# Attention with its normalisation moved from the exponentials to the product, and the reciprocals brought to rows through DRAM

## The chip, the cores and the metric

The kernel runs on one core of a Trainium2 chip. The metric is the device time of one execution in microseconds; lower is better. Five engines matter: TensorE (PE, with its weight loads PEld), VectorE (DVE), ScalarE (ACT), GpSimd (POOL), and SyncE (SP), whose queue issues nearly all transfers.

## The reference

Three stages follow each other. The first is causal attention with a decay over 4 batches of 8 heads, 576 rows and 64 columns; the change is in it. The other two are dense layers over 2304 tokens, 512 to 2048 to 512, with a swish and then a prelu.

```
scores = scale * q k^T + (cum_i - cum_j),  causal
attn = exp(scores - max(scores))
attn = attn / (sum(attn) + 1e-9)
x = attn v          # then [2304, 512]
h = x w_in;  g = h * sigmoid(1.702 h);  x = g w_out
h = x w2_in; g = max(h, 0) + alpha * min(h, 0);  out = g w2_out
```

## The kernel before

**Units.** Attention works on pairs of heads: 4 batches x 4 pairs. Each pair's 576 query rows are cut into a chunk of 256 rows (two tiles of 128) and one of 320 (two tiles of 128 and one of 64 that holds both heads), 32 chunks in all. `chunk` makes scores in PSUM, reduces and masks them on VectorE (L891) into `e`, and takes exponentials in place on ScalarE (L900), which also gives the row sums in `ms`. Then each tile adds 1e-9 to its sums (L905, L909), takes reciprocals (L911), and scales `e` in place by a per-row scalar (L917 on ScalarE, L919 on VectorE or GpSimd). `chunk2`, called one chunk later, transposes `e` on TensorE (L952), copies the transposes to `eT` (L513, L515), multiplies them with v (L966) into one PSUM buffer, and copies the product, which is transposed (columns are query rows), into the ring `xr` (L979). The PSUM pool for that product holds one buffer.

**Background.** The first dense layer (`gemm1`, L1008) works on blocks of 256, 320, 256, 320 and 384 rows as soon as all four pairs of heads have delivered their columns of `xr`; it needs `xh` and `xl`, the high and low parts of `xr`, and weights prepared on all engines. The last 768 rows go through `tail` (L1031). Its matmuls fill TensorE between the attention's.

**Order.** Nothing is ordered by the program's text. `Plan.plan` places all operations by a list schedule with costs and due times; `Plan.run` then emits them in planned order, so each engine's stream is fixed. In the plan a transfer takes 540 ns of its queue, ends 750 ns after a start-up of 1500 ns and its bytes, and its users may start after its `lag` on top of that. Operations of `back` (priorities 1000 to 2000, gemm1) carry a planned penalty if they could start, in nanoseconds the third number of `TRIES`; the first is the penalty for switching the matmul mode, within the second. In the first 130 us `Plan.run` puts filler matmuls on the identity (L484) where the plan leaves TensorE idle.

Of the kernel before, what the change touches and what calls it, by code (L numbers as in the profile page):

```python
# [7 lines left out]
F32 = mybir.dt.float32  # L8
# [4 lines left out]
ALU = mybir.AluOpType  # L13
# [14 lines left out]
TMODE = 0  # L28
PADC = 8000.0
PAD0, PAD1, PADN, PADM = 1600.0, 130000.0, 220.0, 200.0  # L30
TRIES = [(800.0, 3000.0, 200.0)]
QUEUE = {"SP": "SP", "ACTQ": "ACT"}


# [215 lines left out]
def kernel(  # L250
# [13 lines left out]
    nc = tc.nc  # L264

    B, H, S, D = q.shape
    NT, DM = out.shape
    DFF = w1_in.shape[1]
    P = 128
    BH = B * H  # L270
    NP = H // 2
# [12 lines left out]
    RING = 1152  # L284
    SPLIT = 256
# [16 lines left out]
    plan = Plan()  # L302
    E = {"PE": nc.tensor, "DVE": nc.vector, "ACT": nc.scalar, "POOL": nc.gpsimd, "SP": nc.sync, "ACTQ": nc.scalar}
# [3 lines left out]
    dram = ctx.enter_context(tc.tile_pool(name="dram", bufs=1, space=bass.MemoryType.DRAM))  # L307
# [4 lines left out]
    tscr = dram.tile([P, KEPT, WSLOT], F32, name="tscr")  # L312
    w2scr = dram.tile([P, NPAIR, WSLOT], F32, name="w2scr")
    cscr = dram.tile([BH, 2, S], F32, name="cscr")
    region = {}

    order_of = {
# [17 lines left out]
    def sb(reg, nm, slots, shape, dt=F32, after=()):  # L335
        p = Pool(slots, after)
        p.make = lambda i: open_region(reg).tile(shape, dt, name=f"{nm}{i}", tag=f"{nm}{i}")
        return p
# [45 lines left out]
    xr = region["p1"][1].tile([P, KT, RING], F32, name="xr")  # L384
    p1_pools = [p_xh, p_xl, p_gg, p_xr]

    att = region["att"][1]
# [4 lines left out]
    p_z = sb("att", "Z", 2, [P, 2, 2, 64], F32R)  # L392
    bm = att.tile([P, 2], F32, name="bm")
    p_raw = sb("att", "raw", 3, [P, S])
    p_tk = sb("att", "tk", 1, [P, S])

    p_ka = sb("att", "KA", 2, [P, 2, S], F32R)
    p_kb = sb("att", "KB", 2, [P, 1, S], F32R)
    p_qa = sb("att", "QA", QS, [P, 2, S], F32R)
    p_vr = sb("att", "VR", 2, [P, NKT, 2, D])  # L400
    p_ms = sb("att", "ms", 4, [P, 16])
    p_e0 = sb("att", "ea", 2, [P, 6 * P])
    p_e2 = sb("att", "eb", EB, [P, 2, 3 * P])
    p_e3 = sb("att", "ec", EB, [P, 2, 4 * P])
    p_e4 = sb("att", "ed", EB, [P, 5 * P])
    p_et = sb("att", "eT", ET, [P, 640])
    att_pools = [p_z, p_raw, p_tk, p_ka, p_kb, p_qa, p_vr, p_ms, p_e0, p_e2, p_e3, p_e4, p_et]

    banks = [psum.tile([P, 512], F32, name=f"bk{i}") for i in range(8)]

# [83 lines left out]
    lfT = lambda: xr[:, 0, RING - S - NKT * BH:RING - S].rearrange("p (t r) -> p t r", r=BH)  # L494

    b_id, b_mask, b_mask2, b_cum, b_alpha = Buf(), Buf(), Buf(), Buf(), Buf()
    DMA = lambda nbytes: [("SP", nbytes / 360.0)]

    def c_dve(n, fast=False):
        return n / (1.92 if fast else 0.96) + 68.0  # L500
# [10 lines left out]
    def copy(e, dst, src):  # L511
        if e == "ACT":
            nc.scalar.copy(dst, src)  # L513
        else:
            E[e].tensor_copy(dst, src)  # L515
# [10 lines left out]
    def a_out(n):  # L526
        return [("ACT", c_act(n, True)), ("DVE", c_dve(n), BC + WO_ * n)]
# [73 lines left out]
    every = slice(None)  # L601
# [10 lines left out]
    def filled(nm, p):  # L612
        return [fill[nm, len(p.bufs) - 1]] if len(p.bufs) <= p.n else []
# [8 lines left out]
    for part, (lo, hi) in enumerate(((0, SPLIT), (SPLIT, S))):  # L622
        ts_ = [t for t in range(NKT) if lo <= t * P < hi]
        pri = -80 if part == 0 else A0 + P1PRI
# [23 lines left out]
        cs = slice(lo, hi)  # L648
# [13 lines left out]
        [(b_cc, 0)],  # L662
        ("vr", p_vr, lambda x: x[64:P, NKT - 1], 2 * D, 0.0, every),
        ("ed", p_e4, lambda x: x[:, S:], 64, 0.0, every),
    )
    for i in range(2):
        set_rows("dk", p_kb, [i], lambda i=i: p_kb.tiles[i][:, 0], S, -40, [(b_cc, 0)], 0, 64)
# [165 lines left out]
    def a_scale(n):  # L833
        return [("DVE", c_dve(n, True) + 62.0, SC_D, True), ("ACT", c_act(n) + 105.0, SC_A), ("POOL", 280.0 + 2.55 * n, SC_P, True)]

    def chunk(u, q0, q1, pri):
        kh, kl, dk, qh, ql, qo, z = (u[x] for x in ("kh", "kl", "dk", "qh", "ql", "qo", "z"))
        pr = lambda c: range(2 if c > SPLIT else 1)
        ms = Buf(p_ms)
        n = q1 - q0  # L840
        tiles = [(t, t * P, min(P, S - t * P)) for t in range(q0 // P, (q1 + P - 1) // P)]
        view, eb = {}, {}
        if not q0:
            e0 = Buf(p_e0)
        for j, (t, a, w) in enumerate(tiles):
            ext = a + w
# [12 lines left out]
            step = ext if ext <= 512 else ext // 2  # L859
# [43 lines left out]
            last.clear()  # L903
            if w < P:
                plan.add([("DVE", 75.0, 0.0, True)], lambda e: nc.vector.scalar_tensor_tensor(  # L905
                    ms.ap[:, 10:11], ms.ap[:, 10:11], 1e-9, ms.ap[:, 11:12], op0=ALU.add, op1=ALU.add
                ), [(ms, ("s", 11))], [(ms, ("s", 10))], pri)
            else:
                plan.add([("DVE", 70.0, 0.0, True)], lambda e, j=j: nc.vector.tensor_scalar_add(ms.ap[:, 6 + 2 * j:8 + 2 * j], ms.ap[:, 6 + 2 * j:8 + 2 * j], 1e-9), (), [(ms, ("s", 6 + 2 * j)), (ms, ("s", 7 + 2 * j))], pri)  # L909
            cs = [6 + 2 * j, 7 + 2 * j] if w == P else [10]  # L910
            plan.add([("DVE", 85.0)], lambda e, cs=cs: nc.vector.reciprocal(ms.ap[:, cs[0]:cs[-1] + 1], ms.ap[:, cs[0]:cs[-1] + 1]), (), [(ms, ("s", c)) for c in cs], pri)  # L911
            for i, c in enumerate(cs):
                ks = [(eb[t], (t, i, x)) for x in range(0, ext, step)]
                def sc_(e, t=t, i=i, c=c, ext=ext):
                    x = view[t, i](0, ext)
                    if e == "ACT":
                        nc.scalar.mul(x, x, ms.ap[:, c:c + 1])  # L917
                    else:
                        E[e].tensor_scalar_mul(x, x, ms.ap[:, c:c + 1])  # L919
                plan.add(a_scale(ext), sc_, [(ms, ("s", c))], ks, pri)  # L920
        return dict(u=u, q0=q0, q1=q1, pri=pri, view=view, eb=eb)

    last = []

    def chunk2(x):
        u, q0, q1, pri, view, eb = (x[i] for i in ("u", "q0", "q1", "pri", "view", "eb"))
        b, hp, vr = u["b"], u["hp"], u["vr"]
        n = q1 - q0
        pb = Buf(ps_v)
        nt = (q1 + P - 1) // P  # L930
        for t in range(nt):
            s0 = max(q0, t * P)
            m = q1 - s0
            qt = [j for j in (range(2) if not q0 else (2, 3)) if j >= t]
            w = len(qt) * P
            if not q0:
                plans = [[(j, hh) for hh in range(2) for j in qt]]
            elif t < 3:
                plans = [[(j, 0) for j in qt] + [(4, 0)], [(j, 1) for j in qt]]
            elif t == 3:  # L940
                plans = [[(3, 0), (4, 0), (3, 1)]]
            else:
                plans = [[(4, 0)]]
            et = Buf(p_et)
            o = 0
            for blocks_ in plans:
                pt = Buf(ps_e)
                c1 = P * len(blocks_)

                def turn(e, pt=pt, blocks_=blocks_, t=t):  # L950
                    for i, (j, hh) in enumerate(blocks_):
                        nc.tensor.transpose(pt.ap[:, i * P:(i + 1) * P], view[j, hh](t * P, t * P + P), ident)  # L952

                plan.add([("PE", 111.0 * len(blocks_))], turn, [b_id, *{id(eb[j]): eb[j] for j, _ in blocks_}.values()], [pt], pri, mode=TMODE,
                    pad=(pt, lambda pt=pt: pt.ap[:, :P], 0))
                plan.add(a_out(c1), lambda e, pt=pt, et=et, c1=c1, o=o: copy(e, et.ap[:, o:o + c1], pt.ap[:, :c1]), [pt], [(et, o)], pri)
                o += c1

            def av(e, et=et, t=t, s0=s0, m=m, w=w):
                if not q0:  # L960
                    l = [(0, s0 - q0, n, 0), (1, s0 - q0, n, m)]
                else:
                    l = [(0, s0 - q0, n, 0), (1, n - 64, n, w + 64)] + ([(1, s0 - q0, n - 64, w + P)] if w else [])
                seen = set()
                for hh, x0, x1, c0 in l:
                    nc.tensor.matmul(  # L966
                        pb.ap[64 * hh:64 * hh + 64, x0:x1], vr.ap[:, t, hh], et.ap[:, c0:c0 + x1 - x0],
                        start=t == 0 and hh not in seen, stop=t == nt - 1, skip_group_check=True, tile_position=(0, 64 * hh),
                    )
                    seen.add(hh)  # L970

            plan.add([("PE", max(4 * m / 2.4, 230.0))], av, [vr, et, *u["fvr"]], [pb], pri, mode=2,
                pad=(pb, lambda: pb.ap[:, :P], 0) if t == 0 else None)
        t0 = col0(b, q0)
        x = t0
        while x < t0 + n:
            y = min(t0 + n, (x // RING + 1) * RING)
            keys = [XR.setdefault((hp, i % (RING // 64)), Buf()) for i in range(x // 64, y // 64)]
            plan.add(a_out(y - x), lambda e, x=x, y=y: copy(e, xr[:, hp, x % RING:x % RING + y - x], pb.ap[:, x - t0:y - t0]), [pb], keys, pri)  # L979
            x = y  # L980


# [184 lines left out]
    step = 0  # L1167
# [28 lines left out]
    for no, (b, hp, cs_) in enumerate(seq):  # L1196
        us = units[no] if no in units else operands(no, step)
        for unit, c_ in zip(us, cs_):
            q0, q1 = CH[c_]
            pend.append((chunk(unit, q0, q1, A0 + step), col0(b, q0) + q1 - q0 if hp == NP - 1 else 0))  # L1200
            step += 1
            if len(pend) > 1:
                x, t = pend.pop(0)
# [29 lines left out]
    for k in range(NM):  # L1233
        WO[k] = wb = Buf(wo[k >= WO0])
        pri = 1500.0 + k
        w = exact(out_rows(w1_out, k), pri)
# [4 lines left out]
    for i, (t0, n) in enumerate(in_turn):  # L1241
        base = 2000.0 + 100 * i
        py = [Buf(ps_y) for _ in range(KT)]
        for k in range(NM):
            h, lo = stream(h1scr, [(b_g1, (j, k)) for j in crossing(t0, n, p1_parts)], k, t0, n, base + k - 60)
# [56 lines left out]
    for p in range(NPAIR):  # L1302
        TS[p] = sw = Buf(wS)
        pri = 5000.0 + p
# [59 lines left out]
    for gi in range(len(groups)):  # L1364
        t0 = groups[gi][0]
# [140 lines left out]
```

## Time and profile before

| | before |
|---|---|
| median of three runs | 953.04 us (951.09 to 956.74) |
| profiled execution, its own time | 951.31 us |
| its span, first to last instruction | 949.6 us |
| TensorE busy | 939.9 us |
| VectorE busy | 739.8 us |
| ScalarE busy | 561.2 us |
| GpSimd busy | 31.2 us |
| mean granted TensorE clock | 0.998 |

Busy time is the union of an engine's instructions; matmuls overlap, so a busy TensorE need not be TensorE at its peak. A short instruction's duration may overlap the start of the next on the same engine.

### The profile page before, as it was taken

To read this page: it belongs to the slowest core of one execution; us is meant where nothing else is said; L and a number is where in the kernel's file an instruction comes from. 1 tells how busy PE (TensorE), PEld (TensorE's weight loads), DVE (VectorE), ACT (ScalarE), POOL (GpSimd) and SP (SyncE) were. 2 spreads that over 40 slices of the span, in tenths; PEclk is the share of its full clock that TensorE was granted. 3 is DMA by queue.
4 is the path that set the end of the run, shared out by engine and by line. 5 is a ranking of instruction groups with operands and counts; after the bars stand their busy time and mean duration, and the time that the engine had idled before them with its cause. 6 is when DMAs were issued, how large, how long until landed. Compare 5 with 4: busy or idle time off the path is not lost.

```text
span 949.6 us, 18126 instructions
## 1 busy us (share of the span) xinstructions
PE 939.9 (99%) x6517; PEld 873.0 (92%) x6517; DVE 739.8 (78%) x1771; ACT 561.2 (59%) x1238; POOL 31.2 (3%) x46
## 2 busy tenths in 40 slices
PE   8999999999999999999999999999999999999998
PEld 6789898889899999988888988999999999999998
DVE  5999997877759658755768876979569878898987
ACT  6999976777664538556776774556466623221212
POOL 1000010201001000000000000000000000000000
PEclk9999999999999999999999999999999999999999
DMA  7777764343211546558896784787638594443423
GB/s 151 172 185 190 180 158 97 85 92 73 59 52 65 183 159 226 157 174 327 299 323 198 257 257 151 257 307 288 244 124 319 187 398 164 139 150 96 155 79 100
DMA packets 179035, 172.78 MB, mean 182 GB/s; under 512 B 98320, under 2 KB 153760, under 8 KB 176640
## 3 DMA queue, kind: packets, MB, share of 16 engines
q1 hardware_dynamic: 178928, 171.61, 57.9%
q8 instruction: 51, 0.84, 0.4%
q14 instruction: 40, 0.33, 0.1%
q10 hardware_dynamic: 16, 0.01, 0.0%
HBM read 107.71 MB, written 63.85 MB: 181 GB/s over the span
## 4 chain that ended last, share of the span: by engine, by line
PE 89%; DVE 5%; DMA 1%; issue 0%; ACT 0%; DVEq 0%; SPq 0%; ACTq 0%
PE bk L1031 25%; PE bk L1252 21%; PE bk L1434 19%; PE bk L1008 12%; PE bk L966 4%; PE bk L952 4%; PE bk L878 3%; PE bk L872 1%; DVE w L518 1%; DVE wc L688 1%; DMA raw<-in_k_dram 1%; DVE eT L515 0%; DVE wc L687 0%; DVE tk L719 0%; DVE eb L891 0%
## 5 line engine op out<-in xcount | busy, mean ns | idle before, releaser
L1031 PE MATMUL bk<-x,wS 128*128 128x384 f32 x912 | 160.4, 334 | 0.0
L1031 PEld LDWEIGHTS bk<-x,wS 128*128 128x128 f32 x912 | 158.2, 188 | 0.7 <-DVE lx L1057 0.5
L1008 PE MATMUL bk<-xh,w 128*128 128x320 f32 (+2 forms) x640 | 150.2, 310 | 0.1
L1252 PE MATMUL bk<-lh,w 128*128 128x512 f32 (+1 forms) x640 | 146.9, 368 | 0.0
L1252 PEld LDWEIGHTS bk<-lh,w 128*128 128x128 f32 x640 | 112.7, 189 | 19.8
L1008 PEld LDWEIGHTS bk<-xh,w 128*128 128x128 f32 x640 | 108.9, 189 | 4.5 <-issue 1.7
L1008 PE MATMUL bk<-xl,w 128*128 128x320 f32 (+2 forms) x320 | 97.0, 303 | 0.4 <-DVE xl L518 0.4
L518 DVE TENSOR_TENSOR ll<-lx,lh 128x512 fp32r<-128x512 f32 (+1 forms) x80 | 50.9, 636 | 40.0 <-PE bk L1252 26.1
L1252 PE MATMUL bk<-ll,w 128*128 128x512 f32 (+1 forms) x320 | 81.2, 368 | 0.0
L513 ACT CAST x<-x 128x768 fp32r<-128x768 f32 (+3 forms) x41 | 33.4, 825 | 67.5 <-PE bk L1434 54.9
L1434 PE MATMUL bk<-wS,x 128*128 128x256 f32 x567 | 70.5, 283 | 0.0
L1218 ACT ACTIVATE lx<-lx 128x512 f32<-128x512 f32 (+1 forms) x80 | 46.9, 588 | 39.5 <-DVE ll L518 34.6
L1434 PEld LDWEIGHTS bk<-wS,x 128*128 128x128 f32 x567 | 69.1, 192 | 0.0
L1434 PE MATMUL bk<-wS,lh 128*128 128x256 f32 x378 | 68.7, 283 | 0.0
L1252 PEld LDWEIGHTS bk<-ll,w 128*128 128x128 f32 x320 | 57.0, 189 | 9.6
L1008 PEld LDWEIGHTS bk<-xl,w 128*128 128x128 f32 x320 | 60.5, 189 | 0.7 <-DVE xl L518 0.7
L513 ACT CAST lh<-x 128x768 fp32r<-128x768 f32 (+3 forms) x29 | 23.2, 805 | 62.9 <-PE bk L1434 48.3
L518 DVE TENSOR_TENSOR x<-x,x 128x768 fp32r<-128x768 f32 (+3 forms) x59 | 55.9, 979 | 4.1 <-ACT x L513 3.1
L1434 PEld LDWEIGHTS bk<-wS,lh 128*128 128x128 f32 x378 | 59.0, 192 | 0.0
L513 ACT COPY lx<-bk 128x384 f32<-128x384 f32 x72 | 34.3, 481 | 38.6 <-PE bk L1031 25.6
L1434 PE MATMUL bk<-wS,ll 128*128 128x256 f32 x189 | 53.5, 283 | 0.0
L513 ACT CAST lh<-lx 128x512 fp32r<-128x512 f32 (+1 forms) x68 | 38.9, 572 | 16.8 <-PE bk L1252 16.3
(204 smaller groups left out, 1976.4 us busy)
## 6 DMA issues: line engine op xcount, KB each, us to landing
h2scr<-lx SPq DMA_DIRECT2D x96, 192.0 KB, 3.9
wraw<-in_moe_w_in_dram SPq DMA_DIRECT2D x32, 512.0 KB, 5.6
wraw<-in_moe_w_out_dram SPq DMA_DIRECT2D x32, 512.0 KB, 6.3
lx<-h1scr SPq DMA_DIRECT2D x64, 256.0 KB, 4.2
x<-h2scr SPq DMA_DIRECT2D x32, 512.0 KB, 3.8
w2scr<-wS SPq DMA_DIRECT2D x5, 1792.0 KB
tscr<-wS SPq DMA_DIRECT2D x4, 1792.0 KB, 5.8
wS<-tscr SPq DMA_DIRECT2D x4, 1792.0 KB, 10.4
```

What stands on the lines that cost most here:

```text
L513: nc.scalar.copy(dst, src)
L518: E[e].tensor_tensor(dst, a, b, op=ALU.subtract)
L688: plan.add(a_sub(n), lambda e: E[e].tensor_tensor(wi(), wi(), low(), op=ALU.add), [raw], [w], pri)
L872: nc.tensor.matmul(o, x, y, start=i == 0, stop=i == 3)
L878: nc.tensor.matmul(pms[hh].ap[:, f0:f0 + c1 - c0], l, y.ap[r, c0:c1], start=i == 0, stop=i == 3, skip_group_check=True)
L952: nc.tensor.transpose(pt.ap[:, i * P:(i + 1) * P], view[j, hh](t * P, t * P + P), ident)
L966: nc.tensor.matmul(pb.ap[64 * hh:64 * hh + 64, x0:x1], vr.ap[:, t, hh], et.ap[:, c0:c0 + x1 - x0], start=t == 0 and hh not in seen, stop=t ...
L1008: nc.tensor.matmul(ph.ap[:, :n], w.ap[:, a, c, :], x[c // 2].ap[:, c % 2, :n], start=(c == 0 and j == 0), stop=(c == KT - 1 and j == 2))
L1031: nc.tensor.matmul(out.ap[:, :XH], wt(a, c), x.ap[:, b, c, :], start=(st and c == 0 and i == 0), stop=(c == 1 and i == 2), skip_group_chec ...
L1218: plan.add([("ACT", c_act(n))], lambda e: nc.scalar.activation(g.ap[:, :n], raw.ap[:, :n], AF.Gelu_apprx_sigmoid), [raw], [g], pri)
L1252: nc.tensor.matmul(py[d].ap[:, :n], w[:, a, d * P:(d + 1) * P], (lo if x else h).ap[:, :n], start=(k == 0 and (a, x) == (0, 0)), stop=(k = ...
L1434: nc.tensor.matmul(py[j].ap[:, t * HF:(t + 1) * HF], x.ap[:, q:q + P], w[:, o, a, :], start=(k == 0 and t == 0 and c == 0), stop=(k == NPA ...
```

## The change

The scaling of `e` is left out, and the transposed product is multiplied instead. Its columns are query rows, so the factor must lie along the columns, equal in the 64 partitions of a head. For that each chunk's sums go to `rc` (128 x 32, of which 4 or 5 columns are used; columns ordered by head), get 1e-9 added and are inverted there. Four VectorE transpositions of 32x32 turn `rc` into rows in `rt`. A transfer writes 4 or 5 rows of 128 to `rscr` in DRAM, and two or four transfers read them back into `rr`, each repeated over the 64 partitions of a head. The copy of the product to `xr`, planned before on ScalarE or VectorE, is a VectorE multiplication with `rr`. The plan gives the write a lag of 3000 ns and the reads 1500 ns. The penalty on gemm1 goes from 200 to 0.

```diff
-TRIES = [(800.0, 3000.0, 200.0)]
+TRIES = [(800.0, 3000.0, 0.0)]
...
+    rscr = dram.tile([BH, 5 * P], F32, name="rscr")
...
+    p_rr = sb("att", "RR", 3, [P, S - SPLIT])
+    p_rc = sb("att", "rc", 3, [P, 32])
+    p_rt = sb("att", "rt", 3, [P, P])
...
+    DMAR = lambda nbytes: [("SP", nbytes / 360.0)]
...
+        ("rc", p_rc, lambda x: x[:, :], 32, 0.0, every),
...
-                    ms.ap[:, 10:11], ms.ap[:, 10:11], 1e-9, ms.ap[:, 11:12], op0=ALU.add, op1=ALU.add
+                    ms.ap[:, 10:11], ms.ap[:, 10:11], 0.0, ms.ap[:, 11:12], op0=ALU.add, op1=ALU.add
...
-            else:
-                plan.add([("DVE", 70.0, 0.0, True)], lambda e, j=j: nc.vector.tensor_scalar_add(...)
-            cs = [6 + 2 * j, 7 + 2 * j] if w == P else [10]
-            plan.add([("DVE", 85.0)], lambda e, cs=cs: nc.vector.reciprocal(...)
-            for i, c in enumerate(cs):
-                ks = [(eb[t], (t, i, x)) for x in range(0, ext, step)]
-                def sc_(e, t=t, i=i, c=c, ext=ext):
-                    x = view[t, i](0, ext)
-                    if e == "ACT":
-                        nc.scalar.mul(x, x, ms.ap[:, c:c + 1])
-                    else:
-                        E[e].tensor_scalar_mul(x, x, ms.ap[:, c:c + 1])
-                plan.add(a_scale(ext), sc_, [(ms, ("s", c))], ks, pri)
+        nc_ = 5 if q0 else 4
+        ks = [(ms, ("s", 6 + c)) for c in range(nc_)]
+        rc, rt, rr, rs, row = Buf(p_rc), Buf(p_rt), Buf(p_rr), Buf(), 2 * (u["b"] * NP + u["hp"]) + (q0 > 0)
+        frc = filled("rc", p_rc)
+
+        def inverse(e):
+            nc.vector.tensor_scalar_add(rc.ap[:, :4].rearrange("p (h j) -> p j h", h=2), ms.ap[:, 6:10].rearrange("p (j h) -> p j h", j=2), 1e-9)
+            if q0:
+                nc.vector.tensor_scalar_add(rc.ap[:, 4:5], ms.ap[:, 10:11], 1e-9)
+
+        plan.add([("DVE", 75.0 * (nc_ - 3), 0.0, True)], inverse, [*ks, *frc], [rc], pri)
+        plan.add([("DVE", 100.0)], lambda e: nc.vector.reciprocal(rc.ap[:, :nc_], rc.ap[:, :nc_]), (), [rc], pri)
+
+        def turn(e):
+            for g in range(0, P, 32):
+                nc.vector.transpose(rt.ap[:32, g:g + 32], rc.ap[g:g + 32])
+
+        plan.add([("DVE", 4 * 85.0)], turn, [rc], [rt], pri)
+        plan.add(DMAR(nc_ * 512), lambda e: E[e].dma_start(rscr[row, :nc_ * P].rearrange("(c n) -> c n", c=nc_), rt.ap[:nc_, :]), [rt], [rs], pri, 3000.0)
+        for x, w in ((0, 2 * P), (2 * P, 64))[:1 + (q0 > 0)]:
+            for hh in range(2):
+                plan.add(DMAR(256 * w), lambda e, x=x, w=w, hh=hh: E[e].dma_start(
+                    rr.ap[64 * hh:64 * hh + 64, x:x + w], rscr[row, 2 * x + hh * w:2 * x + hh * w + w].partition_broadcast(64),
+                ), [rs], [(rr, (x, hh))], pri, 1500.0)
...
-            plan.add(a_out(y - x), lambda e, x=x, y=y: copy(e, xr[...], pb.ap[:, x - t0:y - t0]), [pb], keys, pri)
+            plan.add([("DVE", c_dve(y - x))], lambda e, x=x, y=y: nc.vector.tensor_tensor(
+                xr[:, hp, x % RING:x % RING + y - x], pb.ap[:, x - t0:y - t0], rr.ap[:, x - t0:y - t0], op=ALU.mult
+            ), [pb, rr], keys, pri)
```

## Rows read from the trace of the kernel before

**Rows 1.** Stretches: busy us (instructions) of PE, PEld, DVE, ACT, POOL; clock; DMA share.

```profile
0.00:60.00 60.00, 55.82 (x429) 43.16 (x430) 46.86 (x182) 49.50 (x136) 5.92 (x20) 0.97 0.74 160
...
60.00:120.00 60.00, 59.50 (x524) 53.28 (x523) 59.92 (x199) 57.27 (x155) 4.80 (x5) 1.00 0.76 190
...
120.00:285.00 165.00, 163.98 (x1461) 147.19 (x1461) 121.09 (x448) 115.69 (x338) 14.26 (x14) 1.00 0.37 88
```

**Rows 2.** Timeline of TensorE: start, duration, line, instructions; idle before and its releaser.

```profile
20.54 1.41 PE L484 MATMUL bk<-ident 128*128 128x128 f32 x8
21.74 1.49 PE L952 MATMUL bk<-ident,ea 128*128 128x128 f32 x6
23.02 1.06 PE L484 MATMUL bk<-ident 128*128 128x128 f32 x4
...
51.68 0.83 PE L484 MATMUL bk<-ident 128*128 128x128 f32 x6
...
75.85 1.60 PE L484 MATMUL bk<-ident 128*128 128x128 f32 x12
...
111.27 0.42 PE L1008 MATMUL bk<-xl,w 128*128 128x320 f32 x1 [0.45 <-DVE xl L518]
...
187.19 0.88 PE L952 MATMUL bk<-ident,ea 128*128 128x128 f32 x6 [1.02 <-DVE eT L515]
```

**Rows 3.** Busy in 0 to 300 us: L919 (DVE, POOL), L917 (ACT), copies to xr.

```profile
0.00:300.00 300.00, 37.28 (x95) 7.07 (x10) 0.99 0.52 122
...
0.00:300.00 300.00, 23.11 (x39) 0.99 0.52 122
...
L513 ACT COPY xr<-bk 128x320 f32<-128x320 f32 (+1 forms) x23 | 9.3, 402 | 15.3 <-PE bk L966 15.3
...
L515 DVE COPY xr<-bk 128x256 f32<-128x256 f32 (+1 forms) x9 | 3.9, 438 | 4.3 <-PE bk L966 4.3
```

**Rows 4.** Timeline of VectorE around short instructions, 79 to 82 us.

```profile
79.16 0.77 DVE L719 STREAM_TRANSPOSE tk<-raw 128x576 f32<-128x576 f32 x1
...
80.99 0.16 DVE L909 TENSOR_SCALAR ms<-ms 128x2 f32<-128x2 f32 x1
81.05 0.42 DVE L687 TENSOR_SCALAR wc<-wc 128x512 int32<-128x512 int32 x1
```

**Rows 5.** Transfers issued 20 to 120 us (KB each, us to landing); last, KB's issue times.

```profile
wraw<-in_moe_w_in_dram SPq DMA_DIRECT2D x16, 512.0 KB, 5.6
h1scr<-gg SPq DMA_DIRECT2D x16, 128.0 KB, 3.9
...
raw<-in_k_dram SPq DMA_DIRECT2D x21, 72.0 KB, 3.2
...
L798 SPq DMA_DIRECT2D KB<-cscr x16: 493/541/1122, 26.3 to 237.0; - x16
```

**Rows 6.** Timelines: last exponentials of two chunks, copies to xr, first of gemm1.

```profile
32.05 0.19 ACT L900 ACTIVATION_READ_ACCUMULATOR ea<-ea,ms 128x1 f32 x1
...
38.80 0.41 DVE L515 COPY xr<-bk 128x256 f32<-128x256 f32 x1
...
39.97 0.38 PE L1008 MATMUL bk<-xh,w 128*128 128x256 f32 x1
...
81.39 0.25 ACT L900 ACTIVATION_READ_ACCUMULATOR ea<-ea,ms 128x1 f32 x1
...
86.06 0.41 ACT L513 COPY xr<-bk 128x320 f32<-128x320 f32 x1
...
89.69 0.36 ACT L513 COPY xr<-bk 128x256 f32<-128x256 f32 x1
```

**Rows 7.** SyncE's timeline, and who its queue waited for (us, times, longest).

```profile
27.95 4.97 SPq L715 DMA_DIRECT2D raw<-in_k_dram x4
33.02 3.66 SPq L715 DMA_DIRECT2D raw<-in_q_dram x4
...
SPq L1014 <- ACT gg L513: 42.1, 23, 7.7
```

More of the change, by code (lines that the diff above doesn't have):

```diff
@@ L406 @@
     p_et = sb("att", "eT", ET, [P, 640])
-    att_pools = [p_z, p_raw, p_tk, p_ka, p_kb, p_qa, p_vr, p_ms, p_e0, p_e2, p_e3, p_e4, p_et]
+    p_rr = sb("att", "RR", 3, [P, S - SPLIT])
+    p_rc = sb("att", "rc", 3, [P, 32])
+    p_rt = sb("att", "rt", 3, [P, P])
+    att_pools = [p_z, p_raw, p_tk, p_ka, p_kb, p_qa, p_vr, p_ms, p_e0, p_e2, p_e3, p_e4, p_et, p_rr, p_rc, p_rt]
     banks = [psum.tile([P, 512], F32, name=f"bk{i}") for i in range(8)]
@@ L905, in chunk @@
                 plan.add([("DVE", 75.0, 0.0, True)], lambda e: nc.vector.scalar_tensor_tensor(
-                    ms.ap[:, 10:11], ms.ap[:, 10:11], 1e-9, ms.ap[:, 11:12], op0=ALU.add, op1=ALU.add
+                    ms.ap[:, 10:11], ms.ap[:, 10:11], 0.0, ms.ap[:, 11:12], op0=ALU.add, op1=ALU.add
                 ), [(ms, ("s", 11))], [(ms, ("s", 10))], pri)
-            else:
-                plan.add([("DVE", 70.0, 0.0, True)], lambda e, j=j: nc.vector.tensor_scalar_add(ms.ap[:, 6 + 2 * j:8 + 2 * j], ms.ap[:, 6 + 2 * j:8 + 2 * j], 1e-9), (), [(ms, ("s", 6 + 2 * j)), (ms, ("s", 7 + 2 * j))], pri)
@@ L910, in chunk @@
-            cs = [6 + 2 * j, 7 + 2 * j] if w == P else [10]
-            plan.add([("DVE", 85.0)], lambda e, cs=cs: nc.vector.reciprocal(ms.ap[:, cs[0]:cs[-1] + 1], ms.ap[:, cs[0]:cs[-1] + 1]), (), [(ms, ("s", c)) for c in cs], pri)
-            for i, c in enumerate(cs):
-                ks = [(eb[t], (t, i, x)) for x in range(0, ext, step)]
-                def sc_(e, t=t, i=i, c=c, ext=ext):
-                    x = view[t, i](0, ext)
-                    if e == "ACT":
-                        nc.scalar.mul(x, x, ms.ap[:, c:c + 1])
-                    else:
-                        E[e].tensor_scalar_mul(x, x, ms.ap[:, c:c + 1])
-                plan.add(a_scale(ext), sc_, [(ms, ("s", c))], ks, pri)
@@ L921, in chunk @@
-        return dict(u=u, q0=q0, q1=q1, pri=pri, view=view, eb=eb)
+        nc_ = 5 if q0 else 4
[6 more added lines that the diff above has]
+                nc.vector.tensor_scalar_add(rc.ap[:, 4:5], ms.ap[:, 10:11], 1e-9)
@@ L923 @@
+        for x, w in ((0, 2 * P), (2 * P, 64))[:1 + (q0 > 0)]:
[3 more added lines that the diff above has]
+                ), [rs], [(rr, (x, hh))], pri, 1500.0)
+        return dict(u=u, q0=q0, q1=q1, pri=pri, view=view, eb=eb, rr=rr)
     last = []
     def chunk2(x):
-        u, q0, q1, pri, view, eb = (x[i] for i in ("u", "q0", "q1", "pri", "view", "eb"))
+        u, q0, q1, pri, view, eb, rr = (x[i] for i in ("u", "q0", "q1", "pri", "view", "eb", "rr"))
@@ L978, in chunk2 @@
             keys = [XR.setdefault((hp, i % (RING // 64)), Buf()) for i in range(x // 64, y // 64)]
-            plan.add(a_out(y - x), lambda e, x=x, y=y: copy(e, xr[:, hp, x % RING:x % RING + y - x], pb.ap[:, x - t0:y - t0]), [pb], keys, pri)
+            plan.add([("DVE", c_dve(y - x))], lambda e, x=x, y=y: nc.vector.tensor_tensor(
+                xr[:, hp, x % RING:x % RING + y - x], pb.ap[:, x - t0:y - t0], rr.ap[:, x - t0:y - t0], op=ALU.mult
+            ), [pb, rr], keys, pri)
             x = y
```

## Prediction

> **What bounds the kernel now.** The view by stretch comes first, because an average over the span hides that the attention stage (the first 285 us) has two halves [rows 1]. From 60 to 120 us VectorE is busy 59.92 us of 60, ScalarE 57.27 and TensorE 59.50: three engines are full at once. From 120 to 285 us VectorE and ScalarE fall to 121 and 116 us of 165, and TensorE stays at 163.98. The change takes work from VectorE and ScalarE, so the question is how much of TensorE's time they cost.
>
> The TensorE timeline answers it [rows 2]. Matmuls follow each other nearly everywhere: background work of the first product (gemm1, 960 matmuls of the blocks) fills the attention's gaps. What is left are holes. One kind is the filler matmuls on the identity (L484), put where the planner expects TensorE to wait. After 20 us the four that matter last 1.41 + 1.06 + 0.83 + 1.60 = 4.9 us; the tail of each overlaps what follows (the first runs from 20.54, and the next work starts at 21.74, 1.20 later), so about 4.1 us by starts. Three of the four stand directly before transposes of e (L952, as behind the first), that is, where e is not yet scaled. The other kind is idle time: 0.5 us from 60 to 120, mostly the wait for xl at 111.27, and 1.02 us from 120 to 285, all of it the wait for an eT copy of VectorE before 187.19. All holes together are 5.6 us, 0.6% of the kernel. So no relief of the other engines can bring much over that, whatever their busy shares say; what follows 285 us is not touched.
>
> **The change part by part.** *Scaling of e leaves.* There are 144 scalings: 95 on VectorE, 39 on ScalarE, 10 on GpSimd [rows 3]. VectorE loses 37.28 us of durations, ScalarE 23.11. With them go 64 additions and 80 reciprocals. Short VectorE instructions overlap: an addition at 80.99 lasts 0.16 us, but the next starts at 81.05 [rows 4]. So these 144 occupy about 0.07 us each, 10 us together. Scalings overlap the next start less; I take 32 us of the 37.
>
> *The product is scaled instead.* The 32 output copies (23 on ScalarE, 9.3 us; 9 on VectorE, 3.9 us) become 32 VectorE multiplications out of PSUM. A copy took 0.44 us on VectorE [rows 3]; a multiplication of the same 256 or 320 columns is not in the trace. It costs no less than the copy, and I bound it above by the 0.77 of the 576-column transposition [rows 4]. I take 0.44, the row of the same shape: VectorE gains 14 us less the 3.9 it had, +10 (at most +21). ScalarE loses 9.3.
>
> *Reciprocals are turned.* Per chunk (32 of them) come one or two additions, one reciprocal and four 32x32 transpositions: 48 + 32 short operations at 0.07 us make 6 us. The trace has only transpositions of 576 columns, 0.77 us each. The 128 small ones are bounded below by the 0.07 us between short starts (9 us together) and above by the 0.16 us that a short one lasts (20 us) [rows 4]; I take 0.1, 13 us, near the short rows. The Trainium skill ("VectorE: DVE Perf Modes", section on the TRN2 errata) gives (N+151)/0.96 ns for an fp32 tensor-tensor operation of N columns; by that page, as an estimate, 32 columns would cost 0.19 us and the 128 transpositions 24 us, 11 more. The start 0.06 us after the addition's speaks against it for short operations.
>
> VectorE's balance: -32 - 10 + 10 + 6 + 13 = -13 us of the 228 in the three stretches [rows 1]; ScalarE's -32 (23.11 + 9.3) of 222. That is real relief in the full stretch, but it is paid out only through the holes. The transposes of e no longer wait for addition, reciprocal and scaling, so I let the three fillers before L952 (1.20 + about 0.6 + 1.4 = 3.2 us) shrink by three quarters, -2.4, and the waits at 111 and 187 by half, -0.8: **-3.2 us**, bounded by 0 and -5.6.
>
> *Transfers.* Each chunk writes its reciprocals to DRAM and reads them back as rows: 1 + 2 transfers for the 256-row chunk, 1 + 4 for the 320-row one, 128 in all, in SyncE's queue. No such pair is in the trace; transfers near it are [rows 5]. In the loaded stretch 20 to 120 us, h1scr stores land 3.9 us after issue, k loads 3.2; the slowest, weight loads of 512 KB, 5.6. An issue as small as KB's lasts 0.54. So from the last exponential of a 256-row chunk: 0.5 us of short operations, 3.9 for the write, 0.54 and 3.2 for the reads, 8.1 us; two issues more for a 320-row one, 9.2. Below, nothing faster than 0.5 + 2 x 3.2 + 0.54 = 7.4 is to be had from these rows; above, 0.5 + 2 x 5.6 + 0.54 = 12.2. The kernel before had 8.05 us from the last exponential (ending at 81.64) to the copy at 89.69 [rows 6]. The plan reckons 0.5 + (1.5 + 0.75 + 3.0) + (0.54 + 1.5 + 0.2 + 0.75 + 1.5), 10 us: more than the landings say. The multiplication is thus placed behind the landing, and VectorE should not stand on it; if it did, everything in VectorE's order waited with it, copies of eT and reductions of scores first, and TensorE behind those. The price is that the product leaves PSUM about 2 us later. In the steady part the gemm1 backlog hides that: the block begun at 111 us [rows 2] had its last copy at 86.06 [rows 6]. Without it each chunk would pay up to 2 us. At the start nothing hides it: gemm1 begins at 39.97, and half of its inner dimension needs the fourth pair's product, copied at 38.80. That pair's exponentials end at 32.24; with 8.1 us the product is there at 40.3, by the plan at 42. I take 2 to 3 us late, half covered by attention work: **+1.5 us**, between 0 and 5.
>
> *SyncE's queue.* The write waits for VectorE, the reads wait for the write, and behind them stand the q, k, v and weight loads and the h1scr stores. SyncE is full early: eight k and q loads take 4.97 + 3.66 us from 27.95, 1.1 each [rows 7]. Some 24 new issues at 0.54 us in the first 60 us are 13 us. Loads are made well ahead of use, so most is covered; without that cover it would be the 13 us. I take **+1.0 us**, between 0 and 13.
>
> *The planner's constant* that held gemm1 back by 200 ns is 0, so slices may be cut differently. No row prices it; it can close holes (at most the 5.6 us) or open as many. I take 0, between ends equally far.
>
> Sum against the profiled execution (span 949.6 us, its own time 951.31): 951.31 - 3.2 + 1.5 + 1.0 = 950.6. That execution lies 1.7 us below the median of 953.04, and three runs spread over 5.7 us, so the median to expect is 951, -0.2%. What a measurement of this kernel can tell from no change is about 0.5%, 4.8 us.
>
> **The rivals.** *A, the forecast:* bound by TensorE, small holes traded; 948 to 956 us.
> *B, scaling's path was the cost:* all holes go and neither start nor queue pays: 951.3 - 5.6 = 945.7; with the start's own fillers shortened too, 941 to 948. For it: fillers stand before L952. Against: the longer path is in the plan itself.
> *C, VectorE stands on the rows (the other side):* landings reach the 5.6 us of the weight loads that share the engines: 12.2 us against the planned 10. VectorE, with 0.08 us idle from 60 to 120, passes 2.2 us on to TensorE in half of some 12 chunks until 120 us: +13 - 3.2, 961. It decides once the pair takes over 10 us. For it: DMA engines 74 to 76% busy until 120 us [rows 1]. Against: 3.2 to 3.9 us for most.
> *D, the queue:* each early read holds SyncE for the write's 3.9 us, loads slip past their lead, and gemm1 begins 10 us later: 951.3 - 3.2 + 10 = 958. SyncE shows such holding now: h1scr stores waited 42.1 us in 23 places for ScalarE, up to 7.7, with others behind them [rows 7]. The Trainium skill ("DMA: Bandwidth & Descriptors", section "Anatomy of one DMA") has the rule that the issuing sequencer makes a semaphore wait before dispatch, not the DMA engine; by it every dependent read stops its queue. Against D: a landing planned long lets other transfers stand between write and reads.
>
> **How the numbers follow.** A 0.45, B 0.27, C 0.16, D 0.12. Faster by over 0.5% (under 948.3): B and a little of A, 0.29. Slower (over 957.8): C and most of D, 0.25. Same: 0.46. The likeliest case alone reaches from 948 to 956; for 8 in 10 the range takes in most of B, C and D: 943 to 963.
>
> **What would show it.** Right: VectorE and ScalarE fall by some 13 and 32 us before 300 us while TensorE's idle and filler time changes by a few; multiplications start without waiting for RR; gemm1 begins 1 to 3 us later. B: fillers after 20 us nearly gone. C: VectorE idle before multiplications, released by a DMA. D: gaps between SyncE's loads, and TensorE waiting for operands or weights before 60 us. The sum is wrong altogether if TensorE's new order opens holes that have nothing to do with the old ones.

## The result, and the profile after

The changed kernel takes 963.98 us (962.97 to 966.31, four runs) against 953.74 before: ratio 1.0116, 95% interval 1.0081 to 1.0150. It is slower by 10 us between the medians, 11 by the ratio, and lies just outside the range. Its profiled execution took 966.31 us with a span of 964.6, 15.0 more than the 949.6 of before.

The stretches come first, with the columns of [rows 1]:

```profile
0.00:60.00 60.00, 51.00 (x385) 39.52 (x387) 43.19 (x167) 43.61 (x119) 7.68 (x24) 0.94 0.70 152
60.00:120.00 60.00, 55.78 (x467) 48.20 (x462) 51.01 (x163) 47.70 (x121) 10.58 (x9) 0.94 0.78 195
120.00:285.00 165.00, 162.55 (x1424) 142.24 (x1422) 117.34 (x450) 105.99 (x330) 11.00 (x10) 1.00 0.45 110
```

VectorE and ScalarE got the relief: 16 and 25 us less in the three stretches than in [rows 1]. Part of ScalarE's is only work that comes later, since the last product of the attention leaves PSUM at 297.80 us instead of 285.40; over the whole execution VectorE is busy 19.0 us less and ScalarE 15.0. TensorE could not use it. It is busy 269.3 us of 285 where it was 279.3, so 10 us more are idle. The granted clock fell as well, 0.97 to 0.94 and 1.00 to 0.94. Two stretches of ten microseconds hold that fall:

```profile
40.00:50.00 10.00, 7.45 (x46) 5.53 (x47) 8.36 (x22) 6.86 (x18) 3.57 (x3) 0.66 0.70 168
...
70.00:80.00 10.00, 7.48 (x40) 6.40 (x42) 8.84 (x29) 8.16 (x21) 1.43 (x1) 0.66 0.85 229
```

A mean of 0.66 is a stretch spent for the most part at the lower level of 1.2 GHz. Both come with TensorE's idle time, as its timeline shows (columns of [rows 2]):

```profile
38.17 0.58 PE L770 MATMUL bk<-ident,r 128*128 128x128 f32 x3
42.55 0.98 PE L770 MATMUL bk<-ident,r 128*128 128x128 f32 x3 [3.79 <-DVE KA L523]
...
47.77 0.42 PE L969 MATMUL bk<-ident,ec 128*128 128x128 f32 x1
47.98 0.42 PE L969 MATMUL bk<-ident,eb 128*128 128x128 f32 x1
...
48.92 0.27 PE L969 MATMUL bk<-ident,ec 128*128 128x128 f32 x1
49.03 0.27 PE L969 MATMUL bk<-ident,ed 128*128 128x128 f32 x1
49.06 0.37 PE L1027 MATMUL bk<-xh,w 128*128 128x256 f32 x1
...
75.87 0.47 PE L969 MATMUL bk<-ident,ec 128*128 128x128 f32 x1 [1.05 <-ACT eT L518]
```

After 3.79 us without work the same transposes follow 0.21 us apart, from 48.9 us on 0.11. Two stretches at 0.66 lose 20 x 0.34 = 6.8 us of full clock, about 1 us of it while TensorE stood idle anyway; before had one, from 20 to 30 us at 0.83, 1.7 us. So of the 15 us of the span 10 to 11 are idle time and about 4 the clock. (By the two pages TensorE's busy time grew by 4.2 us, from 939.9 to 944.1, although 30 filler matmuls ran where before had 58; that is not broken down further.) This execution is the slowest of the four, with a mean clock of 0.992 where the others have 0.995 or 0.996, so the clock weighs more in it than in the median. The first gemm1 matmul is at 49.06 us instead of 39.97 [rows 6].

What the engines stood for in the first 310 us is in the list of waits (us, times, longest):

```profile
ACT wc L691 <- DMA wraw<-in_moe_w_in_dram: 7.2, 5, 3.1
...
DVE xr L996 <- DMA RR<-rscr: 2.6, 4, 1.1
```

```profile
SPq L1033 <- ACT gg L518: 24.0, 18, 4.9
SPq L932 <- DVE rt L929: 12.3, 10, 2.2
```

In the kernel before SyncE's first row was, over the same 310 us:

```profile
SPq L1014 <- ACT gg L513: 53.1, 28, 7.7
```

The multiplications hardly wait for their rows. New is that ScalarE waits for these weights; before has no such row. SyncE's wait for ScalarE at the h1scr stores, which I take as its spare time, fell from 53.1 us to 24.0 (the 42.1 of [rows 7] are those of the first 290 us, where 10.8 are left). Little of it lay where TensorE's new holes are: in the first 120 us it was 4.7 us before and is 2.2 now. In SyncE's and ScalarE's timelines one case reads:

```profile
62.59 1.14 SPq L935 DMA_DIRECT2D RR<-rscr  x1
63.83 0.53 SPq L1033 DMA_DIRECT2D h1scr<-gg  x1
64.40 2.46 SPq L935 DMA_DIRECT2D RR<-rscr  x3
66.96 0.63 SPq L825 DMA_DIRECT2D VR<-in_v_dram  x1
67.64 1.15 SPq L821 DMA_DIRECT2D VR<-in_v_dram  x2
68.89 1.00 SPq L686 DMA_DIRECT2D wraw<-in_moe_w_in_dram  x2
```

```profile
72.63 0.67 ACT L692 ACTIVATE wraw<-wraw 128x512 int32<-128x512 uint32 x1
74.79 0.66 ACT L691 ACTIVATE wc<-wraw 128x512 f32<-128x512 f32 x1 [1.49 <-DMA wraw<-in_moe_w_in_dram]
75.35 0.85 ACT L518 COPY eT<-bk 128x384 f32<-128x384 f32 x2
```

SyncE issues from 62.59 to 69.89 us with gaps of 0.04 to 0.10 us; the weight loads stand behind four reads and three loads of v. ScalarE stands for a weight until 74.79, the eT copy comes behind it in its order, and the transpose at 75.87 waits for that copy.

The new operations by form:

```profile
L929 DVE STREAM_TRANSPOSE rt<-rc 32x32 f32<-32x32 f32 x128 | 25.4, 198 | 1.4
...
L996 DVE TENSOR_TENSOR xr<-bk,RR 128x320 f32<-128x320 f32 x16 | 7.8, 488 | 8.7 <-PE bk L983 6.6 <-DMA RR<-rscr 1.7 <-issue 0.2
L996 DVE TENSOR_TENSOR xr<-bk,RR 128x256 f32<-128x256 f32 x16 | 6.6, 414 | 9.7 <-PE bk L983 4.3 <-ACT eT L518 3.8 <-DMA RR<-rscr 0.9
```

And the 96 reads (issue duration in ns, minimum, median, maximum): 57 us of SyncE's queue by the median, and 9 more for the 32 writes of 0.29.

```profile
L935 SPq DMA_DIRECT2D RR<-rscr x96: 444/591/1822, 30.0 to 295.0; - x96
```

### The profile page after: what moved, and what is told of

It reads as the page before. It is cut to its first block, busy times and chain, and to the rows that moved or that the text cites. A ratio compares the mean times of both kernels' runs of the same rounds, so it can differ in the third digit from the quotient of the medians.

```text
span 964.6 us, 18209 instructions
## 1 busy us (share of the span) xinstructions
PE 944.1 (98%) x6489; PEld 871.1 (90%) x6489; DVE 720.8 (75%) x1721; ACT 546.2 (57%) x1202; POOL 41.0 (4%) x55
## 4 chain that ended last, share of the span: by engine, by line
PE 79%; DVE 3%; ACT 1%; DMA 1%; issue 1%; SPq 1%; DVEq 0%
PE bk L1050 22%; PE bk L1271 20%; PE bk L1453 19%; PE bk L1027 10%; PE bk L983 3%; PE bk L884 2%; PE bk L969 2%; PE bk L878 1%; DMA wraw<-in_moe_w_out_dram 1%; DVE ea L897 0%; DMA RR<-rscr 0%; DVE lx L1063 0%; DVE rt L929 0%; SPq L1033 0%; DVE wc L694 0%
## 5 line engine op out<-in xcount | busy, mean ns | idle before, releaser
L1027 PE MATMUL bk<-xh,w 128*128 128x320 f32 (+2 forms) x640 | 148.1, 311 | 1.8 <-POOL w L523 0.5
L518 ACT COPY gg<-bk 128x320 f32<-128x320 f32 (+2 forms) x65 | 27.0, 417 | 48.4 <-PE bk L1027 32.1
```

Of the source, the lines that this page charges most:

```text
L1027: nc.tensor.matmul(ph.ap[:, :n], w.ap[:, a, c, :], x[c // 2].ap[:, c % 2, :n], start=(c == 0 and j == 0), stop=(c == KT - 1 and j == 2))
```

## The experiments

Ratios are to the kernel before, run on the same chip beside each kernel (951.3 to 953.2 us). The theory is rival D of the prediction: SyncE's queue issues loads late. Its rivals are that VectorE stands on rows, the transpositions' time, and the planner's constant. From `e5_indep` on the theory is split: reads stand in the queue until the write has landed (theory 1), or the issues themselves, or what they move, take the time (theory 2).

**Four parts undone, in the changed kernel's order.** `e1_const` keeps all transfers, but multiplies by a constant column (the normalisation is left out):

```diff
-    ... pb.ap[:, x - t0:y - t0], rr.ap[:, x - t0:y - t0], op=ALU.mult), [pb, rr], keys, pri)
+    ... pb.ap[:, x - t0:y - t0], bm[:, 0:1].to_broadcast([P, y - x]), op=ALU.mult), [pb, rr, b_bm], keys, pri)
```

> The changed kernel in its own order of instructions, but the product is multiplied by a constant column (one per partition) instead of the rows read back; all transfers stay. So no instruction waits for the rows. Wait theory (VectorE standing on the rows is the cause, 2.6 us seen directly, the rest passed on and doubled by the clock): most of the loss returns, 953 to 957. Turn theory (four transpositions last 0.8 us where the plan has 0.34): at most 3 us return, 961 to 964. Queue theory (128 transfers delay the loads): 960 to 964. Order theory (the new plan's order has the holes): 962 to 965.

963.59 us, 1.0108 (1.0087 to 1.0129). Without any dependence on rows the loss stays: VectorE's wait for them is not the cause.

`e2_notransfer` also leaves the 128 transfers out:

```diff
-    lambda e: E[e].dma_start(rscr[...], rt.ap[:nc_, :])
+    lambda e: None
-    lambda e, x=x, w=w, hh=hh: E[e].dma_start(rr.ap[...], rscr[...].partition_broadcast(64))
+    lambda e: None
```

> As the run before it, and the 128 transfers of the reciprocals are left out too; their places in the plan stay, so the order of all other instructions is that of the changed kernel. Queue theory: 3 us or more below the run before it, and the weights no longer come late. Wait and turn theories: within 2 us of the run before it. Order theory: 961 to 965.

956.0 us, 1.0029 (1.0015 to 1.0043). The transfers cost 0.79%, 7.5 us. ScalarE's wait for weights goes:

```profile
ACT wc L691 <- DMA wraw<-in_moe_w_in_dram: 0.9, 1, 0.9
```

And TensorE's idle time shrinks. From 60 to 120 us, first `e1_const`, then `e2_notransfer`:

```profile
60.00:120.00 60.00, 55.02 (x481) 47.10 (x481) 52.19 (x164) 49.83 (x129) 10.45 (x9) 1.00 0.81 202
60.00:120.00 60.00, 58.05 (x508) 50.91 (x509) 56.19 (x189) 53.87 (x146) 10.36 (x9) 1.00 0.73 182
```

That is 3.0 us; over the three stretches it is 5.25, of 5.1 between the two spans. The stretches of low clock are not what the transfers cost. The second, from 70 to 80 us, is at 1.00 already in `e1_const`, which takes as long as the changed kernel. The first, from 40 to 50, stays at 0.66 without the transfers, behind the same wait for KA: it belongs to the new order.

`e3_noturn` keeps the transfers and leaves the transpositions out (`rt` holds ones):

```diff
-            for g in range(0, P, 32):
-                nc.vector.transpose(rt.ap[:32, g:g + 32], rc.ap[g:g + 32])
+            return
```

> The changed kernel in its own order, with the 128 small transpositions left out (the rows hold ones, so the product is not normalised); transfers and waits stay. Turn theory: VectorE gets 20 to 25 us back in the attention stage and runs on time, 953 to 957. Wait theory: the rows are sent 0.8 us earlier per chunk, so 960 to 963. Queue and order theories: 962 to 965.

963.53 us, 1.0105 (1.0085 to 1.0126): 25 us less on VectorE bring nothing that can be told apart while the transfers stay. Part of what VectorE gets back it spends on rows, for which it now stands 9.5 us instead of 2.6.

`e4_back200` plans the changed kernel with the old constant, in an order of its own:

```diff
-TRIES = [(800.0, 3000.0, 0.0)]
+TRIES = [(800.0, 3000.0, 200.0)]
```

> The changed kernel planned with the penalty of 200 on the background again; everything else as changed. Order theory, with this constant as its cause: 952 to 957. The other three theories: the order shifts, but the same work and waits stay, 959 to 967.

965.7 us, 1.0127 (1.0103 to 1.0150): not the cause, as far as two different orders can be compared.

**What of a transfer costs.** `e5_indep` (constant column) lets the reads fetch a row written at the start, so that none waits for the write:

```diff
-    rscr[row, 2 * x + hh * w:2 * x + hh * w + w].partition_broadcast(64)
+    cscr[row % BH, 0, :w].partition_broadcast(64)
```

> As in the run with the constant column (the product is multiplied by a column of ones and zeros instead of the reciprocals), the writes stay, and the 96 reads stay too with their places in SyncE's queue, their widths and their descriptors, but they fetch a row of the cumulated decay that was written at the start, so that no read waits in the queue until a write has landed. Theory 1 (the queue stands at the reads until the write has landed, and the loads of weights behind are issued late): 956 to 958 us, near the 956.0 of the run without transfers. Theory 2 (the issues themselves, some 128 more on a queue that has many, or the bytes that they move, cost the time): 962 to 964 us, as with the constant column.

965.07 us, 1.0129 (1.0113 to 1.0146). Theory 1, that the queue stands until the write has landed, falls.

`e6_small` (constant column) has reads of one partition:

```diff
-    rr.ap[64 * hh:64 * hh + 64, x:x + w], rscr[...].partition_broadcast(64)
+    rr.ap[64 * hh:64 * hh + 1, x:x + w], rscr[...].partition_broadcast(1)
```

> As in the run with the constant column, but each read goes to 1 partition instead of 64: the number of issues, their places and their waits for the write stay, a 64th of the descriptors and bytes is left. Theory 1 (the wait in the queue) and the variant of theory 2 in which the number of issues counts: 962 to 964 us. The variant of theory 2 in which the 64 descriptors of a read are what costs, in the issue or in the transfer engines: 956 to 958 us.

957.39 us, 1.0058 (1.0043 to 1.0073). An issue costs 0.25 us instead of 0.59:

```profile
L935 SPq DMA_DIRECT2D RR<-rscr x96: 214/250/917, 29.7 to 285.1; - x96
...
ACT wc L691 <- DMA wraw<-in_moe_w_in_dram: 2.0, 3, 1.0
```

Count, places and waits are the same, so it is the 64 rows: by the issue time, or by the load on the transfer engines. `e9_small3` separates these. Each read becomes three of one row, 72 us of issue with a twentieth of the rows:

```diff
-    E[e].dma_start(rr.ap[64 * hh:64 * hh + 64, x:x + w], rscr[...].partition_broadcast(64))
+    [E[e].dma_start(rr.ap[64 * hh + i:64 * hh + i + 1, x:x + w], rscr[...].partition_broadcast(1)) for i in range(3)][-1]
```

> As in the run with reads of 1 partition, but each read is three such reads (three rows of three neighbouring partitions), 288 instead of 96: product by the constant column, the same order elsewhere. An issue of one row held SyncE's queue for 0.25 us, so that the reads hold it for 72 us in all, against 24 with one row each and some 62 with the 64 rows of the changed kernel; descriptors and bytes are 3 rows each, a twentieth of the 64. If the time that SyncE needs to issue is the cause: 962 to 966 us. If it is what the 64 descriptors do in the transfer engines: 957 to 958.5 us, as with one row each.

971.34 us, 1.0205 (1.0188 to 1.0222), more than I expected. The waits show the same path, larger:

```profile
ACT wc L691 <- DMA wraw<-in_moe_w_in_dram: 15.0, 6, 5.9
```

The time that the reads hold SyncE's queue, 0, 24, 57 and 72 us by the medians, goes with +0.29, +0.58, +1.08 to +1.29 and +2.05%. SyncE's spare time goes the other way: 62.0, 37.5, 24.0 to 29.1 and 12.7 us. So time in the queue, without the 64 rows, is enough to make a loss of this size, and it costs more the fuller the queue is. (That `e9_small3` also has three times as many issues, each with a gap of its own before it, is part of that time.) That it makes the whole loss of the changed kernel is not shown by this; the runs with another queue below speak against it. The Trainium skill ("Perfetto Trace Analysis", section "What "DMA-bound" means") says that a solid track of the issuing sequencer is descriptor generation, not data movement. This case agrees as to the growth from 0.25 to 0.59 us with the rows.

**The rest of the 2.8 us.** `e7_neither` leaves out transfers and transpositions (both edits above, constant column).

> Neither the transfers nor the transpositions: multiplication by the constant column, everything else in its order. It tells what the 2.8 us are that the run without transfers still lacks to the kernel before. If they are the 25 us of transpositions on VectorE: 953 us or less. If they are the order in which the planner laid the work once the scalings were gone (later k and q transposes, no filler matmuls, TensorE at the lower of its two clock levels for longer): 956 us, as without the transfers.

950.74 us, 0.9983 (0.9971 to 0.9996). So the transpositions cost 0.46%, 4.4 us, once the transfers are out of the way; with them there (`e3_noturn`) nothing of it shows. By the three stretches TensorE is idle 2.95 us less here than in `e2_notransfer`. gemm1 begins at 46.17 us here, six later than before, and the time is not longer for it. The wait for KA (2.6 us) and the low clock behind it (0.71 from 40 to 50 us) are here too, so these alone do not make the kernel slower than before.

`e11_noscale` is the kernel before without the scalings of e (the result is not normalised), in its order:

> The kernel before with the 144 scalings of e left out (the output copies and everything else stay, in the order of before, reciprocals and additions included): the upper bound of what the relief of VectorE, ScalarE and GpSimd can bring as long as the order is not planned anew. By the prediction's sum of the holes 948.6 us (3.2 less than the 951.8 of the kernel before); by the rival in which the path of the scaling was the cost 946 us; by the view that TensorE has nothing to gain 951 to 952 us.

949.39 us, 0.9971 (0.9960 to 0.9982), 2.8 us less than before by the ratio: all that the relief brings in the old order, in which the 32 filler matmuls after 20 us keep their places. From 60 to 120 us TensorE has no idle time left:

```profile
60.00:120.00 60.00, 59.95 (x531) 54.20 (x530) 55.82 (x183) 55.38 (x150) 2.58 (x2) 1.00 0.78 191
```

`e15_back0` is the kernel before with the constant at 0.

> The kernel before planned with the constant 0 instead of 200, nothing else changed. By the prediction's term for the constant (0) and by the run of the changed kernel with 200 (no difference): 950 to 954 us. If the constant hides a loss that the changed kernel only partly shows: 955 us or more.

958.2 us, 1.0050 (1.0029 to 1.0070): a miss. The constant alone costs 0.5% there, and nothing measurable in the changed kernel. Its new order has one new hole,

```profile
32.20 0.45 PE L878 MATMUL bk<-KB,ones 64*128 64x384 f32 x2 [2.30 <-DMA KB<-cscr]
```

where the kernel before waits 0.46 us; that is 1.8 of the 4.8 us. A new plan alone is thus worth half a percent, and the runs planned anew below tell less than those in one order.

**Other queues, other plans, fewer transfers.** `e8_pool` issues write and reads from GpSimd:

```diff
-    E[e].dma_start(...)
+    nc.gpsimd.dma_start(...)
```

> The changed kernel in full, but write and reads are issued by GpSimd, which has little else to do, instead of SyncE. The order on TensorE, VectorE and ScalarE is the same. Theory 1 and theory 2 of SyncE's queue alike (whatever the transfers do there): 955 to 958 us, since the queue is as free as without transfers and the product has its reciprocals in time. Rival (the time goes to the transfer engines or to memory, whoever issues, or VectorE must wait for rows that come later from GpSimd): 962 us or more.

960.53 us, 1.0095 (1.0074 to 1.0115). `e10_poolindep` (constant column, independent reads as in `e5_indep`) and `e13_poolfree` (also without writes) take the waits out of GpSimd's queue:

> Writes and reads in GpSimd's queue, as in the run that moved them there, but the reads fetch a row of the cumulated decay that is written at the start, so that GpSimd stands at no landing, and the product is multiplied by the constant column. 64 rows of a read as in the changed kernel. If SyncE's issue time was the cost, and in the moved version GpSimd's waits before its own share of the weights: 955 to 957.5 us. If the transfer engines' load is the cost: 960 to 963 us.

> As the run with independent reads in GpSimd's queue, but the 32 writes are left out as well, so that nothing of the transfers waits for VectorE in GpSimd's queue (there the writes stood 127 us for it); the 96 reads of 64 rows stay, with their bytes, and the product is multiplied by the constant column. If the 7.5 us that the version with independent reads lost were GpSimd's waits before its share of the weights' work: 955.5 to 957 us, as without any transfer (956.0). If they are the load of the reads on the transfer engines and memory, or GpSimd's 0.53 us for each: 958.5 to 960 us.

959.41 us, 1.0078 (1.0060 to 1.0096), and 959.23 us, 1.0063 (1.0042 to 1.0084). Little comes back, though ScalarE waits only 0.8 us for weights in the first. The reads cost GpSimd 0.53 us each:

```profile
L935 POOL DMA_DIRECT2D RR<-cscr x96: 516/532/684, 27.9 to 280.9; - x96
```

A third to a half of a percent, 3 to 5 us, stays against `e2_notransfer`. A part is GpSimd's own time, since it prepares weights too: TensorE's wait for one of them from 60 to 120 us is 1.4 us in all three runs and 0.5 in `e2_notransfer`. How much is the load of 64 rows on the transfer engines stays open; in `e13_poolfree` the first reads also moved up to 14.8 us, among the first loads.

`e12_trueplan` is planned with measured times: a transposition 200 ns, a write 300, a read 600.

```diff
-    plan.add([("DVE", 4 * 85.0)], turn, ...
-    plan.add(DMAR(nc_ * 512), ...
+    plan.add([("DVE", 4 * 200.0)], turn, ...
+    plan.add([("SP", 300.0)], ...
...
-    plan.add(DMAR(256 * w), ...
+    plan.add([("SP", 600.0)], ...
```

> The changed kernel in full, planned with the times that its trace shows: 600 ns of SyncE's queue for a read (planned 182 or 46), 300 ns for a write, 200 ns for each transposition (planned 85). If the cost is that loads which the planner thinks issued in time are late, the planner can now lay them before the reads: 956 to 960 us. If SyncE is simply full until 120 us, whatever the order: 962 us or more.

959.58 us, 1.0080 (1.0066 to 1.0094): the lowest of the versions that keep the whole change, with an interval that overlaps those of `e8_pool` and of the changed kernel, and slower than before. VectorE stands for rows longer in it than in the changed kernel:

```profile
DVE xr L996 <- DMA RR<-rscr: 12.7, 7, 4.6
```

`e14_split` puts the reads on GpSimd in such a plan (`("POOL", 530.0)`):

> The changed kernel in full, planned anew with the times that the traces show: the write in SyncE's queue at 300 ns, the reads in GpSimd's queue at 530 ns each and in the planner's account of GpSimd, a transposition at 200 ns. By the theory that the time of issue in SyncE's queue is the main cost: 955 to 958 us, faster than the changed kernel by some 7 us and not faster than the kernel before, since the transpositions' 4 us stay. By the theory that the transfers cost the same whoever issues them: 960 us or more.

974.13 us, 1.0221 (1.0193 to 1.0250): a miss. In its order GpSimd waits long for the write, and VectorE for the rows:

```profile
POOL RR L935 <- DMA rscr<-rt: 106.8, 18, 21.8
...
DVE xr L996 <- DMA RR<-rscr: 16.7, 7, 4.4
```

That these rows are what it loses by is not shown: `e12_trueplan` stands 12.7 us for them and is the lowest.

`e16_wide` reads both heads at once, 32 reads instead of 96, for which the rows lie in DRAM head by head and a 320-row chunk needs two writes; `e17_wide2` plans that anew with measured times:

```diff
+    rr.ap[:, :n], rscr[row, :].rearrange("(h w) -> h w", h=2)[:, :n].unsqueeze(1).to_broadcast([2, 64, n])
```

> The changed kernel in full and in its order, with fewer and larger transfers: the rows of a chunk lie in DRAM head by head, so that one read of 2 x 64 rows brings a chunk's reciprocals (32 reads instead of 96; a chunk of 320 rows needs two writes, 48 instead of 32). If a read of 128 rows holds SyncE's queue for about 0.94 us (0.25 for one row and 0.34 more for 63 others, twice), the reads take 30 us of the queue instead of 58. By the theory of the issue time that lies near the one-row reads' 24 us: 957 to 960 us. If the rows moved, which are as many as before, are the cost: 962 us or more.

> As the run before (one read for a chunk), planned anew with measured times: a transposition 200 ns, a write 350, a read 950 in SyncE's queue. By the theory of the issue time 955 to 960 us; the transpositions' 4 us and what the order is worth stay. Better than the kernel before only if the order happens to fall well, since the bound of the gain (scalings left out) was 949.4.

999.2 us, 1.0487 (1.0473 to 1.0502), and 994.7 us, 1.0439 (1.0422 to 1.0455). The issues are short as hoped, and the rows come late:

```profile
L942 SPq DMA_DIRECT2D RR<-rscr x29: 493/525/1410, 30.8 to 298.0; - x29
...
  DVE xr L1003: 38.2, 18
```

One is issued at 67.54 and its multiplication stands until 75.02, 7.5 us; in the changed kernel the last read of a chunk is issued from 66.4 to 66.86 and the multiplication starts at 69.02, 2.6 us after. The load differs between these two (DMA share from 66 to 70 us 1.13 and 0.46), so the totals, 38.2 us in 18 waits against 2.6 in 4, say more than the pair. `e18_two` goes back to one read for each head, over all columns of the chunk:

```diff
+    rr.ap[64 * hh:64 * hh + 64, :n], rscr[row, n * hh:n * hh + n].partition_broadcast(64)
```

> The changed kernel in full and in its order, with two reads of 64 rows for every chunk, one for each head, of 256 or 320 columns: 64 reads instead of 96, with the partitions outermost in source and target as in the changed kernel (in the version with one read the outermost step was 2 heads, and its rows came late). A chunk of 320 rows has two writes, 48 in all instead of 32. Reads then hold SyncE's queue for about 64 x 0.59 = 38 us instead of 57, the 16 more writes for 5 to 13. By the theory of the issue time: 960 to 962.5 us, 2 to 4 us less than the changed kernel, and VectorE's wait for rows a few microseconds as there. If one read was late because of the size of its rows and not of its shape: VectorE stands for rows again, 20 us or more, and the time is 980 us or more.

963.44 us, 1.0135 (1.0119 to 1.0152), against the 960 to 962.5 expected. Nothing is won: the two writes that its layout needs in 320-row chunks last 0.64 and 0.60 us, so that reads and writes hold SyncE for 38 + 25 us, against 57 + 9. But VectorE waits 1.7 us where it stood 38.2, so the lateness comes from the shape with the two heads outermost, or from having 128 rows in one transfer, which was not tried apart, and not from the length of a row. The Trainium skill ("DMA: Bandwidth & Descriptors", section "Rules for kernel authors") says that an outermost dimension of c under 16 confines a transfer to at most c engines; the times of the two runs agree with that, and no view here shows which engines took part.

## Why the prediction was wrong

**Holes, -3.2 us:** the size came out, 2.8 without the scalings, but partly by luck. Of the 3.2, 2.4 were to come from shorter fillers, and `e11_noscale` gains with all its fillers in place. The new plan did drop most of them (8 matmuls of 32 after 20 us are left), while new holes opened. The relief of VectorE came, 19.0 us over the whole execution for the 13 forecast; ScalarE's was 15.0 for 32, since the new plan gives it 16 more copies of eT. A multiplication takes 0.41 to 0.49 us for the 0.44 taken.

**SyncE's queue, +1.0 us, between 0 and 13:** this step failed. The transfers cost 7.5 us (`e1_const` against `e2_notransfer`). "Loads are made well ahead of use, so most is covered" had no row behind it, and only the 24 issues of the first 60 us were counted, while 66 us of issue spread to 295. Rival D had the place, at 12% and 958 us, but not the mechanism: reads that do not wait for the write cost as much. How the 7.5 us divide between SyncE's issue time and the load of the rows stays open, since 3 to 5 of them remain when GpSimd issues the transfers.

**Transpositions, 0.1 us each, at no cost in the end:** the second failure. They take 0.198 us, 25.4 together. The estimate that the prediction set aside, 0.19 us by the formula of the Trainium skill for tensor-tensor operations ("VectorE: DVE Perf Modes", section on the TRN2 errata), agrees with the trace. Four in a row start 0.2 us apart, so the addition's 0.06 us was the wrong row to lean on. Without the transfers they cost 4.4 us. TensorE's one long wait, for KA of VectorE, is 3.6 us with them and 2.6 without; the rest of the 2.95 us of idle time is spread over smaller waits.

**The start, +1.5 us:** gemm1 begins 9 us late, not 1 to 3; six of these are in `e7_neither` too, which is no slower than before. **Rows late, rival C:** 2.6 us of waits, no cost seen (1.0108 without them, 1.0116 with), and `e12_trueplan`, in an order of its own, is lower with 12.7. Where rows came very late, 38 us of VectorE's waits went with 35 more microseconds than the changed kernel takes. **The constant:** no difference in this kernel, as taken, but 0.5% in the kernel before.

In one order the parts add up so: scalings out, product multiplied and the new order itself -0.17%, transpositions +0.46, transfers +0.79, waiting for rows +0.08 (too small to tell from nothing), together 1.16%. The share of a part depends on what else is there, as `e3_noturn` shows. The fall of the clock behind idle stretches was not in the sum either: in the profiled execution it took about 4 us beside the idle time.

## What to carry to other kernels

Price a transfer at its issue time in the queue that it joins, over the whole stretch, and look for the spare time of that queue (here SyncE's wait for the stores); "made ahead" is no cover when the queue is full. Before moving work off engines that look full, leave the work out and time it: here that brought 0.3% in the old order, less than the transfers or the transpositions cost. Keep the partitions outermost in a broadcast read (here one read for each head).

## What the runs showed of the hardware

An issue of a read grew from 0.25 us for one row to 0.59 for 64. A 32x32 transposition takes 0.2 us, also behind others of its kind. A read with two heads outermost was waited for until 7.5 us after its issue, one with 64 rows outermost until 2.6, under unequal load; in total VectorE stood 38.2 us for the former and 2.6 or 1.7 for the latter. At the lower of TensorE's two clock levels the same transposes start 0.21 us apart instead of 0.11.
